# Last stage of a linear attention with a soft mixture of experts: divides on VectorE, chained maxima, sums by halves, 51 weight slots, one written order for the tail

## Chip, cores and metric

The kernel runs on one core of a Trainium2 chip. The metric is the device time of one execution in microseconds; the median of three runs of the kernel before is 335.73 us (335.34 to 335.76). All arithmetic is in float32.

## The reference

Attention without softmax: q, k, v are [8 batches, 8 heads, 576 tokens, 64], and a map `phi` makes 256 positive features of each 64. The result x [4608, 512] goes through a soft mixture of 8 experts with 4 slots each (32 slots).

```python
def phi(x):
    proj = np.einsum('bhsd,df->bhsf', x, w_phi)
    proj = proj - np.max(np.abs(proj), axis=-1, keepdims=True)
    return np.concatenate([np.exp(proj), np.exp(-proj)], axis=-1)
q_p, k_p = (phi(q), phi(k))
kv = np.einsum('bhsf,bhsd->bhfd', k_p, v)
z = np.sum(k_p, axis=2)
num = np.einsum('bhsf,bhfd->bhsd', q_p, kv)
den = np.einsum('bhsf,bhf->bhs', q_p, z)[..., None] + 1e-06
x = num / den                        # then [tokens, heads * 64]
logits = x @ phi_moe                 # [4608, 32]
d = softmax(logits, over tokens);  c = softmax(logits, over slots)
slot_input = d.T @ x                 # [32, 512]
for e in range(8):                   # 4 slots each: 512 -> 1024 -> 512
    slot_out[e] = np.maximum(slot_input[e] @ w1[e], 0.0) @ w2[e]
return c @ slot_out                  # [4608, 512]
```

(Here `phi_moe` is the reference's `phi` of the mixture, and the two softmaxes are written short.)

## The kernel before

**Work and stages.** The batches are taken in 4 pairs of 1152 tokens, 9 tiles of 128 tokens; a pair and a head make a unit (32 units, `NU`), and a unit has 3 chunks of 3 tiles. For each block of 4 tiles TensorE projects q and k (L263), VectorE finds the maxima, ScalarE takes the exponents, and TensorE adds k's features times v into `kvp` (L310). Then `num` (psn, L363) multiplies q's features by it; VectorE scales and adds (L374, L379); POOL adds the denominators (`denom`, L386); VectorE inverts them (L390); POOL divides (`divide`, L405) into tiles of x, `xc` for tiles 0 to 3 and 5 to 8 and `xn` for tile 4 in between. When all heads of a pair are divided, x is transposed on TensorE (psx, L706), copied to SBUF (`xcopy`, L710), and multiplied by the mixture's phi into logits (psl, L416). The maximum over tokens, the sum of exponents (`ssum`) and d.T @ x (`acc`, L455) are kept up as running values, rescaled when the maximum moves.

**The last pair.** Of the last pair, the first three of four column blocks of x are transposed and multiplied ahead (`fturn`, `fxcopy`, `flogits`), and their logits are copied to SBUF (`part`, L728). When the last unit is divided, the rest follows in steps whose names begin with z, for c = 0, 1, 2: transposes (`zturn`, L511) and copies (`zcopy`, L516) of the last column block; `zlog`, which brings `part` back into PSUM by a matmul with the identity (`again`, L422) and adds the last block (L416); `zmax`, a negated maximum (L526) and a minimum with the running one (L528); `zexp` (L534); `zco`, the factors of rescaling (L538); `zlt`, which copies the logits to SBUF for the combine weights (L542); `zdt` and `zde`, which turn the exponents back to tokens (L448, L550); `zsum`, the sums d.T @ x (pss, L558); `zup`, which adds them to `acc` (L563); `zss` for `ssum` (L566, L568); `zone`, the maxima across partitions (L571 to L591); `zst` and `zsi`, which transpose `acc` to the slot inputs `phs` (pst, L601, L603, L606). `zspin` (L613) are four matmuls with constants whose results are not read.

**The tail.** Layer 1 (hp, L813) is followed by `hidden` (L857, L858), `picked` (psh, L866, L869), layer 2 (yp, L888), a copy (`slots`, yt, L895), a matmul that adds the partial sums (`slots2`, psy, L899, and its copy by ScalarE, L900), and the outputs: four matmuls (pso, L908), four copies to `o` by VectorE and ScalarE (L912), two DMAs of 384 KB (L913). `lastw` makes the last three groups' combine weights and `cturn` (L879) transposes all of them.

**What sets the order.** The string `ORDER` names one task after another by a letter; `Plan.run` takes the next task of that kind, and what it issues goes to its engine's queue in that order. In the tail a second string, `TAIL`, sets TensorE's order: L is one layer-2 step (8 matmuls, 16 passes), P `picked`, s `slots`, r `slots2`, O one output group. Layer-2 steps are (q, e): 4 quarters of the columns q, 8 experts e.

**Weights.** 64 tiles of 512 KB (32 of layer 1, 32 of layer 2) come by SP's queue (L234). They lie in slots, whose number grows as pools close: `room` gives 30, 33, 39, 42, 43 and 49 slots. The last 6 of the 49 come with the close of pool "c" (`ends`), which holds x and so waits for `zsum`. The last 15 weights reuse slots of layer 1's weights, and so wait for layer 1.

Of the kernel before, what the change touches and what calls it, by code (L numbers as in the profile page):

```python
# [9 lines left out]
F32 = mybir.dt.float32  # L10
# [8 lines left out]
NBP = B // 2  # L19
# [26 lines left out]
PICK = {'xcopy': 'adda', 'kvcopy': 'daad', 'zcopy': 'ada', 'zlt': 'aadaa', 'zde': 'a'}  # L46
# [75 lines left out]
TAIL = "LLLLLPLLLLLLLsLLLrLsrOLLOLLOLLOLLsOrLLOLLOLLOLLsOrOOO"  # L122
# [3 lines left out]
def tile_kernel(ctx: ExitStack, tc, xT, vv, w, phi, w1, w2, cst, out):  # L126
# [13 lines left out]
    stacks = {k: ExitStack() for k in ("x", "c", "u", "q", "v", "mm", "zl", "num")}  # L140
# [61 lines left out]
    ssum = const.tile([128, 1], F32, name="ssum")  # L202
    low = [const.tile([128, 1], F32, name=f"low{i}") for i in range(2)]
# [177 lines left out]

    def denom(u, t):
        if t[0] == 0:
            dn[u] = sm.tile([128, NT], F32, tag="dn", name="dn", bufs=3)
        t = slice(*t)
        nc.gpsimd.tensor_tensor(dn[u][:, t], qe[u][:, 0, t], un[u][:, t, 64], op=ALU.add)  # L386
# [12 lines left out]
    def divide(u, c):  # L399
# [5 lines left out]
        nc.gpsimd.tensor_tensor(x[:, :, h * D:(h + 1) * D], un[u][:, a:b, 0:64],  # L405
# [12 lines left out]

    def again(ps, p):

        for j in range(G):
            nc.tensor.matmul(ps[32 * j:32 * j + 32], ident[:, 32 * j:32 * j + 32], p, start=True, stop=False, skip_group_check=True)  # L422


# [54 lines left out]
    def wexp(n):  # L479
        nc.scalar.activation(slotw(n), slotw(n), AF.Exp)  # L480
# [27 lines left out]
    def zturn(c):  # L508
        ps = fin["x", c] = zbank("r", ("x", c), [128, G, 128], "psx")
        for j in zj(c):  # L510
            nc.tensor.transpose(ps[:, j], tile4(last_of[c], j)[:, (KC - 1) * 128:KC * 128], ident)  # L511

    def zcopy(c, d):
        t = xTtile(("z", c))
        a, b = zj(c)[0], G
        (nc.vector.tensor_copy if d else nc.scalar.copy)(t[:, a:b], fin["x", c][:, a:b])  # L516
        fin["t", c] = {j: t[:, j] for j in zj(c)}

    def zlog(c):
        ps = fin["l", c] = zbank("lr"[c == 2], ("l", c), [128, 128], "psl")  # L520
        again(ps, part[c])
        slotmm(ps, KC - 1, fin["t", c])

    def zmax(c):
        gm = sm.tile([128, 1], F32, tag="gm", name="gm", bufs=3)
        nc.vector.tensor_reduce(gm, fin["l", c], axis=AX, op=ALU.max, negate=True)  # L526
        lw = sm.tile([128, 1], F32, name=f"lw{c}", bufs=1)
        nc.vector.tensor_tensor(lw, gm, fin["lw", c - 1] if c else low[0], op=ALU.min)  # L528
        fin["lw", c] = lw

    def zexp(c):
        fin["e", c] = sm.tile([128, 128], F32, tag="eT", name="eT", bufs=3)
        fin["s", c] = sm.tile([128, 1], F32, tag="es", name="es", bufs=3)
        nc.scalar.activation(fin["e", c], fin["l", c], AF.Exp, bias=fin["lw", max(c, 1)], accum_out=fin["s", c])  # L534

    def zco(i):
        fin["co", i] = sm.tile([128, 1], F32, tag="co", name="co", bufs=3)
        nc.scalar.activation(fin["co", i], fin["lw", 1] if i else low[0], AF.Exp, scale=-1.0, bias=fin["lw", 1 + i])  # L538
# [14 lines left out]
    def zsum(c):  # L553
        if c != 1:
            fin["sum", c // 2] = zbank("lr"[c == 2], ("s", c), [128, DM], "pss")
        ps = fin["sum", c // 2]
        for j in range(G):
            nc.tensor.matmul(ps[32 * j:32 * j + 32], fin["d", c][:, j], tile4(last_of[c], j), start=c != 1, stop=c > 0,  # L558
                             skip_group_check=True)

    def zup(i, h):
        d = slice(h * DH, (h + 1) * DH)
        nc.vector.scalar_tensor_tensor(acc[:, d], acc[:, d], fin["co", i], fin["sum", i][:, d], op0=ALU.mult, op1=ALU.add)  # L563
# [415 lines left out]
```

## Time and profile before

| | |
|---|---|
| median of 3 runs | 335.73 us (335.34 to 335.76) |
| the profiled execution's own time | 336.97 us |
| its span | 335.2 us |
| granted TensorE clock, 270 to 305 | 1.00 |
| start of layer 1 (hp) | 279.64 |
| first output group (pso) | 305.53 |
| instructions | 16723 |

The profile is of one execution. Its span is what the instructions cover; the execution's own time has 1.77 us more, which lie around it. All positions in the text are microseconds from the start of the span. Rows of a timeline have the start, the length, the engine, the line, the operation, the tiles (out<-in) and how many instructions the row holds; in brackets is how long the engine idled before, and what it waited for ("issue" where the profile shows nothing that it waited for). A busy TensorE in such a row may hold short gaps, as ends of matmuls are modelled.

### The profile page before, as it was taken

What the parts mean: (1) busy time and instruction counts of PE and PEld (TensorE: products, weight loads), DVE (VectorE), ACT (ScalarE), POOL (GpSimd) and SP (SyncE); (2) the same over time, 40 slices, a digit from 0 to 9 for tenths busy, and PEclk for the clock granted to TensorE, in tenths of its full rate; (3) what the DMA queues carried; (4) which work ended last, traced back from release to release, by engine and by line L of the source; (5) the groups of instructions that cost most, each with busy time, mean ns of one, the idle gap of its engine ahead of it and who ended that gap; (6) DMA issues with size and microseconds to landing.
All of it is one profiled execution on the core that took longest, in us unless ns stands there. A gap on an engine that the chain in (4) does not pass through costs nothing.

```text
span 335.2 us, 16723 instructions
## 1 busy us (share of the span) xinstructions
PE 321.5 (96%) x7106; PEld 272.1 (81%) x7106; DVE 239.0 (71%) x682; ACT 228.9 (68%) x676; POOL 162.9 (49%) x344
## 2 busy tenths in 40 slices
PE   8999999999999999899999999999999999999980
PEld 4899999999979999898799999979998843376640
DVE  1478788786979888678898877687898665313560
ACT  2899989967886996788688977867886450002450
POOL 1645785863547667542867687237695310200000
PEclk9999999999999999999999999999999999999997
DMA  6647367563745775464557846225525878997997
GB/s 212 198 130 231 106 210 231 169 226 121 283 167 168 231 275 189 168 231 124 168 202 214 307 157 210 92 60 212 173 103 195 316 311 310 414 407 288 367 372 296
DMA packets 23130, 74.12 MB, mean 221 GB/s; under 512 B 2576, under 2 KB 2960, under 8 KB 23056
## 3 DMA queue, kind: packets, MB, share of 16 engines
q1 hardware_dynamic: 23056, 73.05, 62.1%
q8 instruction: 56, 0.92, 1.1%
q14 instruction: 18, 0.15, 0.1%
HBM read 63.60 MB, written 9.44 MB: 218 GB/s over the span
## 4 chain that ended last, share of the span: by engine, by line
PE 92%; DVE 3%; issue 1%; ACT 1%; DVEq 0%; POOL 0%; ACTq 0%; POOLq 0%
PE kvp L310 23%; PE psn L363 21%; PE psq L263 12%; PE psk L263 11%; PE yp L888 5%; PE psx L706 4%; PE hp L813 4%; PE pso L908 3%; PE psl L416 3%; PE pss L455 2%; PE psw L183 1%; PE pss L558 1%; PE psd L448 1%; PE psh L866 1%; DVE xT L710 1%
## 5 line engine op out<-in xcount | busy, mean ns | idle before, releaser
L283 POOL TENSOR_TENSOR vs<-vt,mk 128x520 f32<-128x520 f32 (+3 forms) x128 | 91.5, 730 | 69.1 <-ACT mk L272 52.1
L310 PE MATMUL kvp<-vs,kf 128*64 128x65 f32 (+1 forms) x2304 | 92.6, 229 | 0.0
L310 PEld LDWEIGHTS kvp<-vs,kf 128*64 128x64 f32 x2304 | 81.5, 138 | 7.2 <-issue 2.3
L363 PE MATMUL psn<-kvs,qf 128*64 128x65 f32 x2304 | 80.1, 223 | 0.1
L263 PE MATMUL psq<-xs,wd 64*128 64x128 f32 x576 | 75.7, 280 | 0.9 <-issue 0.9
L363 PEld LDWEIGHTS psn<-kvs,qf 128*64 128x64 f32 x2304 | 73.4, 138 | 3.1 <-issue 1.0
L263 PE MATMUL psk<-wd,xs 64*128 64x128 f32 x576 | 75.8, 280 | 0.1
L263 PEld LDWEIGHTS psq<-xs,wd 64*128 64x128 f32 x576 | 67.5, 187 | 4.0 <-issue 2.3
L263 PEld LDWEIGHTS psk<-wd,xs 64*128 64x128 f32 x576 | 67.3, 187 | 3.0 <-issue 1.6
L268 DVE TENSOR_REDUCE mk<-psk 128x4 f32<-128x512 f32 x72 | 48.4, 675 | 13.8 <-PE psk L263 8.3
L325 DVE TRANSPOSE_TENSOR_REDUCE mts<-psq 128x16 f32<-128x512 f32 x72 | 50.6, 706 | 6.6 <-PE psk L263 2.9
L294 ACT ACTIVATE kf<-psk 128x512 f32<-128x512 f32 x72 | 42.5, 592 | 17.5 <-DVE mk L268 7.6
L330 ACT ACTIVATE qf<-psq 128x512 f32<-128x512 f32 x72 | 42.3, 594 | 8.8 <-DVE dn L390 3.3
L374 DVE TENSOR_TENSOR un<-psn,eq 128x195 f32<-128x195 f32 x96 | 33.0, 350 | 18.4 <-PE psn L363 9.8
L405 POOL TENSOR_TENSOR xc<-un,dn 128x256 f32<-128x256 f32 x64 | 39.2, 614 | 14.2 <-DVE dn L390 11.8
L333 ACT ACTIVATE qf<-psq 128x512 f32<-128x512 f32 x72 | 43.2, 603 | 0.5 <-DVE mts L325 0.5
L297 ACT ACTIVATE kf<-psk 128x512 f32<-128x512 f32 x72 | 42.6, 596 | 0.5 <-DVE mk L268 0.4
L379 DVE TENSOR_TENSOR un<-psn,un 128x195 f32<-128x195 f32 x96 | 32.8, 349 | 1.0
L341 ACT ACTIVATE mh<-mts 32x36 f32<-32x36 f32 x128 | 29.5, 230 | 4.5 <-DVE mts L325 2.6
L347 DVE TENSOR_REDUCE eq<-mh 32x9 f32<-32x36 f32 x128 | 26.2, 205 | 1.5
L271 ACT ACTIVATE mk<-mk 128x4 f32<-128x4 f32 x72 | 15.2, 210 | 12.4 <-DVE mk L268 10.9
L912 DVE COPY o<-pso 128x384 f32<-128x384 f32 x24 | 12.1, 551 | 9.7 <-PE pso L908 9.7
(116 smaller groups left out, 319.5 us busy)
## 6 DMA issues: line engine op xcount, KB each, us to landing
wt<-w SPq DMA_DIRECT2D x64, 512.0 KB, 6.4
xs<-xT SPq DMA_DIRECT2D x36, 512.0 KB, 4.2
vt<-vv SPq DMA_DIRECT2D x32, 325.0 KB, 3.7
out<-o SPq DMA_DIRECT2D x24, 384.0 KB, 4.4
xs<-xT SPq DMA_DIRECT2D x2, 128.0 KB, 2.6
cs<-cst SPq DMA_DIRECT2D x1, 128.0 KB, 3.1
wd<-w SPq DMA_DIRECT2D x1, 64.0 KB, 2.1
phs<-phi SPq DMA_DIRECT2D x1, 64.0 KB, 2.9
```

What stands on the lines that cost most here:

```text
L263: nc.tensor.matmul(ps, l, r, start=True, stop=True)
L268: nc.vector.tensor_reduce(km[b][:, 2], kx[b], axis=AX, op=ALU.max, apply_absolute_value=True)
L283: nc.gpsimd.tensor_tensor(vs[b][:, :, place(b, u, t, o):place(b, u, t, o) + n], v[:, t + o:t + o + n].unsqueeze(1).broadcast_to([128, 2, n ...
L294: nc.scalar.activation(kf[b][:, 1], kx[b], AF.Exp, scale=-1.0)
L297: nc.scalar.activation(kf[b][:, 0], kx[b], AF.Exp)
L310: nc.tensor.matmul(ps[f:f + FE // 2, pn, o:o + m], kf[b][:, pn, NT * u + t - 4 * b, f:f + FE // 2], v2[:, pn, at:at + m], start=(t == 0 an ...
L325: nc.vector.tensor_reduce(mts.rearrange("p r j -> p j r")[:, o:o + 4], qx[b].rearrange("p j (r t) -> p (j r) t", t=32), axis=AX, op=ALU.ma ...
L330: nc.scalar.activation(qf[b][:, 0], qx[b], AF.Exp)
L333: nc.scalar.activation(qf[b][:, 1], qx[b], AF.Exp, scale=-1.0)
L363: nc.tensor.matmul(ps[64 * f:64 * f + 64, j, pn], q2[:, pn, 64 * f:64 * f + 64], kv[:, pn, b2], start=True, stop=True)
L374: nc.vector.tensor_tensor(un[u][:, CH * c:CH * c + CH], nx[s][:, :, 0], e[:, 1].unsqueeze(2).broadcast_to([128, CH, 65]), op=ALU.mult)
L405: nc.gpsimd.tensor_tensor(x[:, :, h * D:(h + 1) * D], un[u][:, a:b, 0:64], dn[u][:, a:b].unsqueeze(2).broadcast_to([128, b - a, 64]), op=A ...
```

## The change

`divider(u)` gives VectorE instead of POOL for `denom` and `divide` of the last unit. The `again` matmuls and the `zlt` copies are gone: `zmax` is now one `tensor_tensor_reduce`, which writes −(psl + part) over `part` and takes the running minimum along. For chunk 2 it adds a tile of zeros instead, since that chunk's `flogits` go into the very PSUM bank of its `zlog`, with no `part` copy before. Each `zmax` takes the result of the one before it. `zexp` reads `part` with scale −1; chunk 0's exponents use the first minimum, those of chunks 1 and 2 the last. `zzero` clears chunk 1's bank.

`zturn` and `zcopy` of chunk 2 are split in two halves, on ScalarE and VectorE; `zsum` of chunks 1 and 2 goes by halves of 256 columns, each half with its `zup`. The transposed tiles of x get a pool of their own ("t"), which closes after the last `zlog`; the slots are now 30, 33, 39, 42, 43, 45 and 51. `ORDER` is rewritten from its 14th line on. The code of the tail goes inside the manually ordered part for all engines; `lastw` first does the transposes, minima, differences and exponents of all three groups, then their sums and divisions; layer 2 goes quarter by quarter, and `TAIL` is another string.

```diff
-PICK = {'xcopy': 'adda', 'kvcopy': 'daad', 'zcopy': 'ada', 'zlt': 'aadaa', 'zde': 'a'}
+PICK = {'xcopy': 'adda', 'kvcopy': 'daad', 'zde': 'a'}
...
-    "bpzLxAHaArItlmKdknomAfygjvhirwfzAravkdmlhijOgcnowqApAcvbdjmwgsfrfltrlkPymvhijwhajnoxdirkvmgznovjcGpwcblfAdmqlrks"
+    "bpzLxAHaAyrmtdjOGmmfkzIKlhAnigfolcpdvarqbwkghnrldvjAmgivMworwAsfAhtvrxiwvknLcfyhjzAljdocikrjngAwmomvlpNkdbqcfwrg"
...
-TAIL = "LLLLLPLLLLLLLsLLLrLsrOLLOLLOLLOLLsOrLLOLLOLLOLLsOrOOO"
+TAIL = "LLLPLLLLLLsLLrLOLLLOLsLLOrLLOLLOLLsLLrOLLOLLOLLsOrOOO"
...
+    def divider(u):
+
+        return nc.vector if u == NU - 1 else nc.gpsimd
...
-        nc.gpsimd.tensor_tensor(x[:, :, h * D:(h + 1) * D], un[u][:, a:b, 0:64],
+        divider(u).tensor_tensor(x[:, :, h * D:(h + 1) * D], un[u][:, a:b, 0:64],
...
     def zlog(c):
-        ps = fin["l", c] = zbank("lr"[c == 2], ("l", c), [128, 128], "psl")
-        again(ps, part[c])
-        slotmm(ps, KC - 1, fin["t", c])
+        if c == 0:
+            fin["l", c] = zbank("l", ("l", c), [128, 128], "psl")
+        ps = fin["l", c]
+        t = {j: fin["t", c][:, j] for j in zj(c)}
+        for j in t:
+            nc.tensor.matmul(ps[32 * j:32 * j + 32], phs[:, KC - 1], t[j], start=c < 2, stop=True, skip_group_check=True)
...
     def zmax(c):
-        gm = sm.tile([128, 1], F32, tag="gm", name="gm", bufs=3)
-        nc.vector.tensor_reduce(gm, fin["l", c], axis=AX, op=ALU.max, negate=True)
-        lw = sm.tile([128, 1], F32, name=f"lw{c}", bufs=1)
-        nc.vector.tensor_tensor(lw, gm, fin["lw", c - 1] if c else low[0], op=ALU.min)
-        fin["lw", c] = lw
+        lw = fin["lw", c] = sm.tile([128, 1], F32, name=f"lw{c}", bufs=1)
+        if c == 2:
+            part[c] = sm.tile([128, 128], F32, tag="lT", name="part", bufs=3)
+        nc.vector.tensor_tensor_reduce(out=part[c], in0=fin["l", c], in1=zero.broadcast_to([128, 128]) if c == 2 else part[c], scale=-1.0, scalar=fin["lw", c - 1] if c else low[0],
+                                       op0=ALU.add, op1=ALU.min, accum_out=lw)
+        lTs[last_of[c]] = part[c]
...
-        nc.scalar.activation(fin["e", c], fin["l", c], AF.Exp, bias=fin["lw", max(c, 1)], accum_out=fin["s", c])
+        nc.scalar.activation(fin["e", c], part[c], AF.Exp, scale=-1.0, bias=fin["lw", c and 2], accum_out=fin["s", c])
...
+    ZS = (0, 0, 2), (1, 0, 1), (1, 1, 2), (2, 0, 1), (2, 1, 2)
...
-            ("u", [("divide", (NU - 1, 2))]), ("c", [("zsum", 2), ("zlog", 2)])]
+            ("u", [("divide", (NU - 1, 2))]), ("t", [("zlog", c) for c in range(NCH)]), ("c", [("zsum", 4)])]
...
-    last("hopen", 0, None, 0.0, hopen, after=[("zsi", 1)] + [("zspin", i) for i in range(NFIN)] + [("zlt", c) for c in range(NCH)], lat=0.0)
+    last("hopen", 0, None, 0.0, hopen, after=[("zsi", 1)] + [("zspin", i) for i in range(NFIN)], lat=0.0)
...
-        l2 = iter([(q, e) for q, n in ((0, 0), (1, 0), (0, 4), (1, 4)) for e in range(n, n + 4)]
-                  + [(q, e) for q in (2, 3) for e in range(NE)])
+        l2 = iter([(q, e) for q in range(4) for e in range(NE)])
```

The first place is VectorE from the last copies of the last pair to the running minima (`dn` the denominators, `gm` a chunk's negated maximum, `lw` the running minimum, `un` the numerators). Before:

```order
L390 RECIPROCAL dn<-dn 128x3
L516 COPY xT<-psx 128x128
L526 TENSOR_REDUCE gm<-psl 128x1
L528 TENSOR_TENSOR lw_6045<-gm,low_134 128x1
L526 TENSOR_REDUCE gm<-psl 128x1
L528 TENSOR_TENSOR lw_6060<-gm,lw_6045 128x1
L526 TENSOR_REDUCE gm<-psl 128x1
L528 TENSOR_TENSOR lw_6064<-gm,lw_6060 128x1
```

After, in the same place:

```order
L396 RECIPROCAL dn<-dn 128x3
L411 TENSOR_TENSOR xc<-un,dn 128x4x64
L411 TENSOR_TENSOR xn<-un,dn 128x64
L411 TENSOR_TENSOR xc<-un,dn 128x4x64
L531 MEMSET psl 96x128
L519 COPY xT<-psx 128x128
L537 ISA part,lw_6026<-psl,part,low_136 128x128
L537 ISA lw_6026 128x1
L519 COPY xT<-psx 128x256
L575 SCALAR_TENSOR_TENSOR ssum<-ssum,co,es 128x1
L537 ISA part,lw_6045<-psl,part,lw_6026 128x128
L537 ISA lw_6045 128x1
```

The three divides have come from POOL. Each `tensor_tensor_reduce` is two instructions, a wide one and one of 128x1, and between the first and the second minimum now stand the copy of a half of chunk 2 and the first step of `ssum`, which needs chunk 0's sum of exponents and its factor from ScalarE. The third minimum follows the second at once.

The second place is TensorE from the last logits to layer 1 (`psl` logits, `psd` exponents turned back, `pss` sums, `psm` maxima across partitions, `pst` slot inputs, `psw` the spins). Before:

```order
L422 MATMUL psl<-part,cs 32x128 x4
L416 MATMUL psl<-xT,phs 32x128 x4
L448 MATMUL psd<-cs,eT 128x128
L574 MATMUL psm<-cs,lw_6064 1x128
L448 MATMUL psd<-cs,eT 128x128
L558 MATMUL pss<-xc,de 32x512 x4
L582 MATMUL psm<-cs,lr 32x1 x4
L448 MATMUL psd<-cs,eT 128x128
L558 MATMUL pss<-xn,de 32x512 x4
L558 MATMUL pss<-xc,de 32x512 x4
L601 MATMUL pst<-ssum,sf 128x1
L603 MATMUL pst<-sf,acc 128x32 x4
```

After:

```order
L422 MATMUL psl<-xT,phs 32x128 x12
L527 MATMUL psl<-xT,phs 32x128 x4
L447 MATMUL psd<-cs,eT 128x128
L566 MATMUL pss<-xc,de 32x512 x4
L583 MATMUL psm<-cs,lw_6052 1x128
L447 MATMUL psd<-cs,eT 128x128 x2
L566 MATMUL pss<-xn,de 32x256 x4
L591 MATMUL psm<-cs,lr 32x1 x4
L566 MATMUL pss<-xn,de 32x256 x4
L566 MATMUL pss<-xc,de 32x256 x8
L610 MATMUL pst<-ssum,sf 128x1
L612 MATMUL pst<-sf,acc 128x32 x4
```

The 12 first logits of chunk 2 now stand right ahead of its last four, with no identity matmuls between; the two last psd stand together, and the sums go by halves. Two of the spins now follow `pst`.

The third place is TensorE at the first outputs (`yp` layer 2, two rows to a step; `psy` the adding up, `pso` an output group). Before:

```order
L899 MATMUL psy<-yt,cs 128x128
L888 MATMUL yp<-wt_6137,sh 32x128 x4
L888 MATMUL yp<-wt_6139,sh 32x128 x4
L899 MATMUL psy<-yt,cs 128x128
L908 MATMUL pso<-ct,yt 128x384 x4
L888 MATMUL yp<-wt_6141,sh 32x128 x4
```

After:

```order
L908 MATMUL yp<-wt_5843,sh 32x128 x4
L908 MATMUL yp<-wt_5845,sh 32x128 x4
L919 MATMUL psy<-yt,cs 128x128
L908 MATMUL yp<-wt_5847,sh 32x128 x4
L908 MATMUL yp<-wt_5983,sh 32x128 x4
L928 MATMUL pso<-ct,yt 128x384 x4
L908 MATMUL yp<-wt_5985,sh 32x128 x4
```

The first output group had both psy of the first two quarters ahead of it, the second of them right before it; now there is one, with a layer-2 step between it and the group, and twelve steps in all before the first output instead of sixteen.

More of the change, by code (lines that the diff above doesn't have):

```diff
@@ L385, in denom @@
         t = slice(*t)
[L386 removed]
+        divider(u).tensor_tensor(dn[u][:, t], qe[u][:, 0, t], un[u][:, t, 64], op=ALU.add)
     def recip(u, t):
@@ L892, in tile_kernel @@
-    yt = slot(spare[2], "yt").rearrange("p (i q c) -> p i q c", i=2, q=4)
-    def slots(q):
-        nc.vector.tensor_copy(yt[:, 0, q], yp[q])
-    def slots2(q):
-        ps = bank([128, COLS], "psy")
-        nc.tensor.matmul(ps, rep, yt[:, 0, q], start=True, stop=True)
-        return nc.scalar.copy(yt[:, 1, q], ps).ins
-    def outputs(q, g):
-        ps = [bank([128, TRI * 128], "pso") for _ in range(G)]
-        c = ct[g // 2][:, g % 2 * TRI * 128:(g % 2 + 1) * TRI * 128]
-        for j in range(G):
-            rows = slice(32 * j, 32 * j + 32)
-            nc.tensor.matmul(ps[j], yt[rows, 1, q], c[rows], start=True, stop=True)
-        for k in range(2):
-            o = slot(next(free), "o")[:, 0:2 * TRI * 128].rearrange("p (k t) -> p k t", k=2)
-            for j in range(2):
-                (nc.scalar.copy if j else nc.vector.tensor_copy)(o[:, j], ps[2 * k + j])
-            nc.sync.dma_start(out[(q * 3 + g) * 2 + k], o)
@@ new lines, in tile_kernel, with cturn, layer2 @@
+        spare = [order[i] for i in range(len(wsrc) - nslot[-1], len(order)) if order[i] < NE * KC]
+        gone = [i if i < nslot[-1] else order[i - nslot[-1]] for i in range(NE * KC, NE * (KC + 2))]
+        free = iter(spare[3:] + gone + keep[0:2])
+        ct = [slot(spare[i], "ct") for i in range(2)]
+        def cturn(i, a, b):
+            nc.vector.transpose(ct[i][:, 0:(b - a) * 128], call[:, 4 * a:4 * b].rearrange("p t s -> p (t s)"))
+        yp = {}
+        def layer2(q, e):
+            if q not in yp:
+                yp[q] = ph[0].tile([128, 512], F32, tag=f"h{q % 2}", name="yp")[:, 0:COLS]
+            for c in range(FC):
+                g, o = 32 * (c % 4), c % 4 * DH + q % 2 * COLS
+                nc.tensor.matmul(yp[q][g:g + 32], sh[e // 4][:, e % 4, c],
+                                 wt[NE * KC + (q // 2 * NE + e) * 2 + c // 4][:, o:o + COLS],
+                                 start=(e == 0 and c < 4), stop=(e == NE - 1 and c >= 4), skip_group_check=True)
@@ new lines, in tile_kernel, with slots, slots2, outputs @@
+        yt = slot(spare[2], "yt").rearrange("p (i q c) -> p i q c", i=2, q=4)
+        def slots(q):
+            nc.vector.tensor_copy(yt[:, 0, q], yp[q])
+        def slots2(q):
+            ps = bank([128, COLS], "psy")
+            nc.tensor.matmul(ps, rep, yt[:, 0, q], start=True, stop=True)
+            return nc.scalar.copy(yt[:, 1, q], ps).ins
+        def outputs(q, g):
+            ps = [bank([128, TRI * 128], "pso") for _ in range(G)]
+            c = ct[g // 2][:, g % 2 * TRI * 128:(g % 2 + 1) * TRI * 128]
+            for j in range(G):
+                rows = slice(32 * j, 32 * j + 32)
+                nc.tensor.matmul(ps[j], yt[rows, 1, q], c[rows], start=True, stop=True)
+            for k in range(2):
+                o = slot(next(free), "o")[:, 0:2 * TRI * 128].rearrange("p (k t) -> p k t", k=2)
+                for j in range(2):
+                    (nc.scalar.copy if j else nc.vector.tensor_copy)(o[:, j], ps[2 * k + j])
+                nc.sync.dma_start(out[(q * 3 + g) * 2 + k], o)
```

206 lines of the change are left out of this document (101 added, 105 removed), and 4 rows, old and new, of the table LETTERS.

## The prediction

> **What bounds the kernel now.** I read the page first, for the engine that is never free, then the windows view for where that stops being so.
>
> ```profile
> span 335.2 us, 16723 instructions
> PE 321.5 (96%) x7106; PEld 272.1 (81%) x7106; DVE 239.0 (71%) x682; ACT 228.9 (68%) x676; POOL 162.9 (49%) x344
> ```
>
> ```profile
> 250.00:260.00 10.00, 9.95 (x218) 8.88 (x218) 8.42 (x25) 6.88 (x22) 5.81 (x13) 1.00 0.48 172
> 270.00:280.00 10.00, 9.11 (x107) 4.86 (x107) 7.22 (x35) 4.51 (x19) 0.27 (x1) 1.00 0.67 254
> 274.40:277.30 2.90, 2.90 (x33) 0.75 (x32) 2.74 (x16) 1.92 (x9) 0.00 (x0) 1.00 0.09 35
> 277.30:305.40 28.10, 26.25 (x418) 14.79 (x414) 9.31 (x43) 1.95 (x4) 1.85 (x2) 1.00 0.99 389
> 305.40:308.00 2.60, 2.60 (x47) 1.44 (x47) 1.02 (x2) 1.13 (x3) 0.00 (x0) 1.00 0.19 68
> 308.00:333.00 25.00, 17.91 (x313) 10.08 (x310) 11.64 (x24) 9.82 (x24) 0.00 (x0) 0.95 0.97 378
> ```
>
> After the window's length stand the busy times of PE, PE's weight loads, DVE, ACT and POOL, then the granted clock, the DMA share and GB/s. TensorE is full until about 270, so up there only less work on it, or a wait, can move the time. Then comes a stage with short instructions (270 to 280), then the expert weights and the output, where the DMA engines are full but for two holes: 274.4 to 277.3 (share 0.09) and 305.4 to 308 (0.19).
>
> What makes the first hole is seen in the waits and the issues of SP's queue:
>
> ```profile
> SPq L234 <- PE pss L558: 8.1, 1, 8.1
> ```
>
> ```profile
> 276.88 7.78 SPq L234 DMA_DIRECT2D wt<-w  x11
> ```
>
> The next weights wait for the slots that pool "c" holds until the last sums (L558) have run. The second hole lies between the last weight and the first output, which is issued here:
>
> ```profile
> 307.10 23.36 SPq L913 DMA_DIRECT2D out<-o  x24
> ```
>
> From there to the end the outputs fill the DMA (0.97), 24 of them in some 25 us, about 1.0 us each, while TensorE hands them over two at a time. So three things set the end: when layer 1 starts, what TensorE waits for until its first output, and how far the DMA is behind then.
>
> **The change part by part.** The profiled execution took 336.97 us with a span of 335.2, so 1.77 lies around the span; it is 1.24 above the median 335.73 of the runs. I work out a difference against the profiled execution and take it off the median.
>
> The stage before layer 1, in the timeline of all engines (start, length, engine):
>
> ```profile
> 268.34 0.61 POOL L405 TENSOR_TENSOR xc<-un,dn 128x256 f32<-128x256 f32 x1 [0.43 <-DVE dn L390]
> ...
> 269.21 0.86 PE L416 MATMUL psl<-xT,phs 128*32 128x128 f32 x24
> ...
> 269.65 0.62 POOL L405 TENSOR_TENSOR xc<-un,dn 128x256 f32<-128x256 f32 x1 [0.29 <-DVE dn L390]
> ...
> 271.34 0.60 ACT L516 COPY xT<-psx 128x512 f32<-128x512 f32 x1
> ...
> 272.47 0.43 PE L422 MATMUL psl<-part,cs 128*32 128x128 f32 x8
> ...
> 272.71 0.40 PE L416 MATMUL psl<-xT,phs 128*32 128x128 f32 x8
> ...
> 273.51 0.16 DVE L528 TENSOR_TENSOR lw<-gm,lw 128x1 f32<-128x1 f32 x1
> ...
> 273.88 0.30 ACT L538 ACTIVATE co<-low,lw 128x1 f32<-128x1 f32 x1
> ...
> 274.38 0.21 DVE L566 SCALAR_TENSOR_TENSOR ssum<-ssum,co,es 128x1 f32<-128x1 f32 x1
> ...
> 274.90 0.38 ACT L534 ACTIVATE eT<-psl,lw 128x128 f32<-128x128 f32 x1
> ...
> 275.45 0.33 PE L448 MATMUL psd<-cs,eT 128*128 128x128 f32 x1
> ...
> 276.00 0.24 ACT L550 COPY de<-psd 128x128 f32<-128x128 f32 x1
> ...
> 276.60 1.04 PE L558 MATMUL pss<-xc,de 128*32 128x512 f32 x8
> 276.85 1.73 DVE L563 SCALAR_TENSOR_TENSOR acc<-acc,co,pss 128x256 f32<-128x256 f32 x4
> ...
> 279.36 0.36 DVE L606 COPY phs<-pst 128x64 f32<-128x64 f32 x2 [0.32 <-PE pst L603]
> ...
> 279.64 2.81 PE L813 MATMUL hp<-wt,phs 128*32 128x512 f32 x24 [0.32 <-DVE phs L606]
> ```
>
> and, for operations that the trace does not have yet, the groups by form of 262 to 280, whose second number is the mean in ns:
>
> ```profile
> L563 DVE SCALAR_TENSOR_TENSOR acc<-acc,co,pss 128x256 f32<-128x256 f32 x4 | 1.7, 478 | 0.1
> ...
> L710 DVE COPY xT<-psx 128x512 f32<-128x512 f32 x2 | 1.4, 692 | 0.6 <-PE psx L706 0.6
> ...
> L477 DVE TENSOR_TENSOR call<-call,cm 128x128 f32<-128x128 f32 x2 | 0.6, 284 | 0.0
> ```
>
> 1. *Up to the last logits, −0.4.* The last divide of 256 columns takes POOL 0.61; on VectorE I price it between 0.28 (a two-input pass over 128 columns) and 0.48 (a three-operand one over 256), and take 0.42, nearer the second, whose width it has. Two of them stand in the row that the transposes wait for: 2 × (0.61 − 0.42) = −0.4 (−0.7 to −0.3). The last identity step is gone: 272.71 − 272.47 = −0.24; the other two are hidden by the copies that TensorE waits for, so I count nothing. Chunk 2's last copy goes in two halves on two engines: a VectorE copy of 512 columns is 0.69, a half some 0.42 by its share, against the 0.6 of a whole one: −0.2. Against this, the 12 first logits of chunk 2 now stand just before the last four: 24 passes of the row at 269.21 are 0.86, so 0.43. That work was TensorE's ahead of the stage and is only moved, but here it is in the way: +0.4 in this place. Sum −0.4. The two part copies that fall away (of ACT) are hidden.
>
> A page bears on the divide: the Trainium skill, "SBUF — State Buffer", section "SBUF: two separate sides", says that a VectorE instruction with two SBUF inputs and a GpSimd instruction that reads SBUF hold one port pair by turns, and the second waits out the first. No row here shows such a wait; by the page the gain of the divides could be lost while POOL works beside them, and the sum below would be −1.2.
>
> 2. *From the last logits to layer 1, +0.2.* Before, 272.71 to 279.64, 6.93. Four pieces. (a) To the last running minimum: before to 273.67, 0.96. After, the three maxima are a chain, and each is two instructions on VectorE: the wide one lies between 0.28 (L477) and 0.48 (L563), I take 0.36, since one operand is in PSUM but only 128 wide; the narrow one like the row at 273.51, 0.16 to 0.21. Between the first and second stand the half copy and the first ssum step (0.21), which waits for exp (0.38) and co (0.30) on ACT. The second maximum so starts late and the third is done about 1.7 after the last logits: +0.7. (b) From there to the last dispatch weights in SBUF (276.24): before 2.57, since ACT does copies and a co between. After, two exps in a row, one psd, one copy: 0.38 + 0.38 + 0.33 + 0.24 and hand-overs of 0.1: 1.4, so −1.2. (c) Sums: halves let the first half be added while the second runs, but chunk 1 and chunk 2 now come together: +0.1. (d) From acc to layer 1: the second half of pst waits for the first phs copy, and two spin passes stand ahead of layer 1: they lie in TensorE's waits (0.32 at 279.64), and cost up to 0.3 each if these are gone: +0.5 with the pst wait. Sum +0.1; I take +0.2. With VectorE's maxima at their upper price, 0.12 and 0.05 more for three, it would be +0.7; at the lower, 0.
>
> 3. *The rewritten order from about 224 to 268, 0.* TensorE idles 0.05 of 10 us there, so nothing is to be had, only lost. I take nothing, bounds −0.2 and +1.5.
>
> Layer 1 so starts at about 279.4.
>
> 4. *Weight slots.* Two slots come free with the transposed x, ahead of the sums; so two 512 KB weights go in the first hole, and all later ones are earlier by what those two took. At the 389 GB/s of the stretch behind it, two of them are 2.7 us, about the 2.64 us of the hole that are idle (2.90 × 0.91).
>
> 5. *Layer 2 up to the first outputs.* TensorE's rows there:
>
> ```profile
> 301.76 1.95 PE L888 MATMUL yp<-wt,sh 128*32 128x128 f32 x62 [0.83 <-issue]
> ...
> 305.11 0.49 PE L899 MATMUL psy<-yt,cs 128*128 128x128 f32 x2 [0.41 <-DVE yt L895]
> 305.53 0.93 PE L908 MATMUL pso<-ct,yt 32*128 32x384 f32 x8
> 306.39 1.08 PE L888 MATMUL yp<-wt,sh 128*32 128x128 f32 x32
> 307.40 1.66 PE L908 MATMUL pso<-ct,yt 32*128 32x384 f32 x8
> 308.99 1.08 PE L888 MATMUL yp<-wt,sh 128*32 128x128 f32 x32
> ```
>
> The wait of 0.41 for yt goes: the new string puts two layer-2 steps between the copy and its psy. −0.41. The steps themselves are all done in both; the first output comes after 12 of them instead of 16, and one psy is put behind it: with two steps to the row of 1.08, that is 2.2 + 0.49 + 0.41 + 0.2 = 3.3 earlier, at some 302.3, without a gain at the end by itself.
>
> Two rows are longer than their work: 0.83 of "issue" before 301.76, and 1.66 for a pso group that took 0.93 at 305.53, so 0.73. The instruction queue explains both:
>
> ```profile
> q8 instruction: 56, 0.92, 1.1%
> ```
>
> ```profile
> q8 instruction: 1, 0.02, 5.0%
> ```
>
> ```profile
> q8 instruction: 1, 0.02, 4.9%
> ```
>
> The first row is the page's: 56 packets, 0.92 MB, 16 KB each. The others are the DMA view of 299.0 to 300.4 and of 305.4 to 306.8; in the 11 us before the first of these there is none. By count, 2 × 7106 instructions over 56 packets are some 127 passes a packet, and between the two stalls TensorE made 62 + 2 + 16 + 2 + 8 + 32 passes and a few. So each stall is TensorE waiting for its own next block of program, fetched late behind full DMA queues. The first stays where it is: weights still load then. The second comes when, by 4, the weights have been in for some 2.6 us, and its fetch is no longer behind them: −0.73.
>
> The Trainium skill, "Runtime: NRT & Kernel Launch", section "Instruction fetch mechanics", has blocks of 16 KiB, as this trace does, and calls the cost of crossing one "mostly hidden". The 0.83 above disagrees. By that sentence there would be no stall to save and the sum would be −0.9.
>
> 6. *Output phase, −0.3.* From the sixth output group on the two strings are equal, so TensorE has the same work from there. What is different is the queue ahead of the DMA:
>
> ```profile
> out<-o SPq DMA_DIRECT2D x2, 384.0 KB, 4.1
> ```
>
> That is the view of 317.0 to 318.4: 4.1 us to landing, of which two outputs' own share is 2.0. With outputs starting some 3 us earlier this backlog is smaller in the middle; at the end three groups come in a burst in either case, and their landing bounds what is left of it. I take −0.3, between 0 and −1.3.
>
> Sum: −0.4 + 0.2 + 0 − 0.41 − 0.73 − 0.3 = −1.6. The profiled execution would come to about 335.3, the median to 334.1.
>
> **The rivals.**
>
> *The end follows the DMA.* From 277.3 on the DMA is full but for the second hole. If what goes into the first hole comes through in full, the end moves by the 2.6 us of it: 333.1. For it: the shares of 0.99 and 0.97. Against it: after the fifth output group the new string has five layer-2 steps and a psy without an output, 2.5 × 1.08 + 0.49 = 3.2 us, in which the 2 us of an output pair run dry; and TensorE's own work up to its last output is not shortened by earlier weights. 16 in 100.
>
> *The second fetch stays late.* Outputs are already on the queues when TensorE asks for that block, or the packets fall elsewhere, and the 0.73 is lost there or at another place: −0.9, 334.8. For it: both stalls came in less than 8 us, so the place counts. Against it: the second fetch comes well after the weights now. 12 in 100.
>
> *What is gained comes back before layer 1.* The maxima at their upper price (+0.7 instead of +0.2) with ssum waiting for ACT, spins without cover, and that fetch late as well: −1.6 + 0.5 + 0.7 = −0.4, 335.3. For it: VectorE is busy 7.22 of 10 us in that stage and its part of the chain is longer now. Against it: (b) is 1.2 of work that is plainly no longer in the way. 18 in 100.
>
> *Slower: the rewritten order makes TensorE wait between 224 and 268.* Every engine follows its list strictly. In the old one TensorE idles 0.05 us in 250 to 260, while VectorE is at 8.42 and ACT at 6.88 of 10. In 270 to 280, where each step waits for another engine, it idles 0.89 of 10. At 0.6 of that rate, a scale or an exponent that comes late in each round, 44 us lose 4.4 × 0.89 × 0.6 = 2.4, and with the −1.6 the time is 336.5. It decides from 1.6 us of holes on. For it: 0.05 us is no slack, and every piece of the list from there on is in a new place. Against it: the sequence of TensorE's own rows is much the same, and the engines beside it have some 1.5 to 3 us of 10 free. 17 in 100.
>
> **How the numbers follow.** 334.1 stands with 37 in 100. About 0.2%, 0.7 us, is what a measurement of this kernel can tell from no change. Faster: the forecast, the DMA rival and the late fetch, 0.65; within: 0.18; slower: 0.17. The range goes from 332.8, a little below the DMA rival, with divides and backlog at their better ends, to 336.3, which takes in the no-change case and the milder half of the slower one.
>
> **What would show it.** In the profile of the changed kernel: TensorE busy over 9.9 of 10 in 250 to 260 (else the slower rival); layer 1 (hp) starting between 279.0 and 279.8; 1.5 to 2 us from last logits to the last minimum; a DMA share over 0.7 in the 3 us that were at 0.09; no wait for yt before the first outputs; one stall of about 0.8 in layer 2 and no long pso row; first output group at about 302.3. I am wrong if hp starts later than 280, if both stalls are there, or if the end moves by another amount than TensorE's last output group does, save for 0.3.

## The result and the profile after

The changed kernel takes 333.5 us (median of 20 runs, 332.35 to 338.26), the kernel before, timed beside it, 335.44 (20 runs, 334.21 to 339.35). The ratio is 0.9942, 95% interval [0.9921, 0.9963]: −1.95 us, between −2.65 and −1.25. Forecast were −1.6. The profiled execution took 333.26 us, with a span of 331.5.

The span alone is 3.7 us shorter, more than the medians. Part of this is not the change's. TensorE's list is the same in both kernels up to about 223, and yet the two traces are apart there already. This is one group of k times v, in the timeline of TensorE, before and after:

```profile
191.42 1.10 PE L310 MATMUL kvp<-vs,kf 128*64 128x65 f32 x32
```

```profile
190.16 1.10 PE L312 MATMUL kvp<-vs,kf 128*64 128x65 f32 x32
```

The profiled execution of before is 1.26 us late at this place, in a part that the change leaves alone; one wait of 0.87 at 135.04 in it, called "issue", was 0.13 in the other. So I compare distances within a trace: from this mark to layer 1, and from layer 1 to the landing of the last output.

The page of the changed kernel, and its windows, cut where its own DMA share changes (length; busy time of PE, weight loads, DVE, ACT, POOL; clock, DMA share, GB/s):

```profile
span 331.5 us, 16703 instructions
PE 318.7 (96%) x7098; PEld 271.1 (82%) x7098; DVE 240.4 (73%) x688; ACT 229.1 (69%) x674; POOL 161.5 (49%) x339
```

```profile
250.00:260.00 10.00, 9.91 (x242) 9.25 (x239) 9.29 (x30) 8.16 (x24) 7.32 (x19) 1.00 0.53 187
270.00:274.60 4.60, 4.08 (x67) 1.95 (x63) 2.66 (x13) 2.88 (x12) 0.00 (x0) 1.00 1.01 397
274.60:276.60 2.00, 2.00 (x30) 1.25 (x30) 1.35 (x4) 0.29 (x1) 0.00 (x0) 1.00 0.36 100
276.60:301.50 24.90, 24.43 (x359) 12.22 (x361) 10.31 (x47) 2.57 (x6) 1.84 (x2) 1.00 1.01 392
301.50:302.90 1.40, 1.40 (x52) 1.20 (x52) 1.00 (x2) 0.86 (x2) 0.00 (x0) 1.00 0.29 111
302.90:328.70 25.80, 19.45 (x369) 11.65 (x366) 11.83 (x25) 9.99 (x25) 0.00 (x0) 0.93 0.95 368
```

TensorE hardly starves in the rewritten order (9.91 of 10). The first hole of the DMA has shrunk from 2.6 idle us to 1.3 (2.00 × 0.64), the second from 2.1 to 1.0. In the outputs the share is 0.95, with a dip to 0.55 from 313 to 315, behind the four layer-2 steps without an output that start at 310.16.

Up to layer 1, in the timeline of all engines of the changed kernel:

```profile
264.34 0.92 PE L365 MATMUL psn<-kvs,qf 128*64 128x65 f32 x24
...
269.48 0.29 DVE L519 COPY xT<-psx 128x128 f32<-128x128 f32 x1 [2.04 <-PE psl L527]
269.69 0.34 DVE L537 CUSTOM_DVE_ANT_0 part<-psl,part,low 128x128 f32<-128x128 f32 x1
...
269.96 0.08 DVE L537 DVE_READ_ACCUMULATOR2_ANT lw<- 128x1 f32 x1
...
270.27 0.37 ACT L519 COPY xT<-psx 128x256 f32<-128x256 f32 x1 [1.28 <-PE psl L527]
...
270.67 0.40 ACT L544 ACTIVATE eT<-part,lw 128x128 f32<-128x128 f32 x1
270.70 0.20 PEld L527 LDWEIGHTS psl<-xT,phs 128*32 128x32 f32 x8
270.70 0.47 PE L527 MATMUL psl<-xT,phs 128*32 128x128 f32 x8
...
271.38 0.22 DVE L575 SCALAR_TENSOR_TENSOR ssum<-ssum,co,es 128x1 f32<-128x1 f32 x1 [0.69 <-ACT co L548]
...
271.90 1.06 PE L566 MATMUL pss<-xc,de 128*32 128x512 f32 x8 [0.36 <-ACT de L556]
...
272.29 0.08 DVE L537 DVE_READ_ACCUMULATOR2_ANT lw<- 128x1 f32 x1
...
278.13 3.21 PE L833 MATMUL hp<-wt,phs 128*32 128x512 f32 x28
```

From the mark to layer 1 it is 87.97 (278.13 − 190.16) where it was 88.22: −0.25. The last minimum is there 1.67 after the last logits (272.29 + 0.08 − 270.70), as forecast.

TensorE in layer 2 and at the first outputs:

```profile
295.50 3.70 PE L908 MATMUL yp<-wt,sh 128*32 128x128 f32 x128
299.13 0.49 PE L919 MATMUL psy<-yt,cs 128*128 128x128 f32 x2
299.55 0.42 PE L908 MATMUL yp<-wt,sh 128*32 128x128 f32 x7
300.12 0.49 PE L908 MATMUL yp<-wt,sh 128*32 128x128 f32 x9 [0.15 <-issue]
300.54 0.93 PE L928 MATMUL pso<-ct,yt 32*128 32x384 f32 x8
301.40 1.52 PE L908 MATMUL yp<-wt,sh 128*32 128x128 f32 x48
302.85 0.93 PE L928 MATMUL pso<-ct,yt 32*128 32x384 f32 x8
303.70 1.52 PE L908 MATMUL yp<-wt,sh 128*32 128x128 f32 x48
305.15 0.93 PE L928 MATMUL pso<-ct,yt 32*128 32x384 f32 x8
```

The yt wait is gone, every pso group takes 0.93, and of the two waits of 0.83 and 0.73 a single one of 0.15 is left. The first output group stands 22.41 after layer 1 started, where it was 25.89. From layer 1 to the last landing (330.53; before, 334.24) it is 52.40 instead of 54.60: −2.20. With the −0.25 ahead of it that is −2.45, inside the interval of the times.

### The profile page after: what moved, and what is told of

It is laid out like the page before. It is cut to its first block, busy times and chain, and to the rows that moved or that the text cites. A ratio compares the mean times of both kernels' runs of the same rounds, so it can differ in the third digit from the quotient of the medians.

```text
span 331.5 us, 16703 instructions
## 1 busy us (share of the span) xinstructions
PE 318.7 (96%) x7098; PEld 271.1 (82%) x7098; DVE 240.4 (73%) x688; ACT 229.1 (69%) x674; POOL 161.5 (49%) x339
## 4 chain that ended last, share of the span: by engine, by line
PE 93%; DVE 2%; ACT 1%; issue 1%; POOL 0%; DVEq 0%; POOLq 0%; ACTq 0%
PE kvp L312 23%; PE psn L365 21%; PE psq L265 12%; PE psk L265 11%; PE psx L717 5%; PE yp L908 5%; PE hp L833 4%; PE pso L928 3%; PE psl L422 2%; PE pss L454 2%; PE psw L183 1%; PE pss L566 1%; PE psh L886 1%; PE psd L447 1%; PE psy L919 1%
## 5 line engine op out<-in xcount | busy, mean ns | idle before, releaser
L411 POOL TENSOR_TENSOR xc<-un,dn 128x256 f32<-128x256 f32 x62 | 38.1, 616 | 11.5 <-DVE dn L396 8.2
```

Source lines behind the costliest of these rows:

```text
L411: divider(u).tensor_tensor(x[:, :, h * D:(h + 1) * D], un[u][:, a:b, 0:64], dn[u][:, a:b].unsqueeze(2).broadcast_to([128, b - a, 64]), op= ...
```

## The experiments

All are changes of one of the two kernels. Times of a run scatter by some 1 us either way, so a ratio says little below 0.3%. The distances in the traces are finer, but each is from one execution. Against the one trace of before, the two distances together (mark to layer 1, layer 1 to last landing) come out 0.3 to 1.4 us better than the times in every kernel, and outside the interval of the times in three: −1.73 for after_49slots, −2.19 for before_newtail_2fewer, −2.62 for after_pooldivide. So the tail in that trace of before may be longer than usual, and comparisons among the other kernels are the safer ones. "Mark" is the same place of k times v as above; "num" is the start of the last num matmul.

| kernel | ratio to before, 95% | mark to layer 1 | num to layer 1 | layer 1 to last landing |
|---|---|---|---|---|
| before | 1 | 88.11 | 12.49 | 54.60 |
| changed | 0.9942 [0.9921, 0.9963] | 87.86 | 13.09 | 52.40 |
| before_newtail | 0.9997 [0.997, 1.0024] | 88.10 | 12.48 | 53.91 |
| after_oldtail | 0.9991 [0.9968, 1.0013] | 87.71 | 13.09 | 54.02 |
| after_49slots | 0.9984 [0.9953, 1.0014] | 87.87 | 13.09 | 53.11 |
| before_2fewer | 1.0007 [0.9976, 1.0039] | 88.72 | 12.48 | 53.95 |
| before_newtail_2fewer | 0.9975 [0.9944, 1.0007] | 88.05 | 12.48 | 52.47 |
| after_pooldivide | 0.9954 [0.9926, 0.9981] | 87.74 | 13.11 | 52.35 |
| after_zsslate | 0.9947 [0.9924, 0.997] | 88.05 | 13.10 | 52.52 |
| after_xt5 | 0.9936 [0.991, 0.9962] | 87.61 | 12.65 | 52.52 |
| after_xt5_zsslate | 0.9921 [0.9896, 0.9945] | 87.21 | 12.65 | 52.54 |

(The mark here is the 1701st pass of k times v, a few passes into the row above. The distance from num is compared among kernels with the same order only, since the changed order puts other work behind the last num.)

### The tail alone: before_newtail

```diff
-TAIL = "LLLLLPLLLLLLLsLLLrLsrOLLOLLOLLOLLsOrLLOLLOLLOLLsOrOOO"
+TAIL = "LLLPLLLLLLsLLrLOLLLOLsLLOrLLOLLOLLsLLrOLLOLLOLLsOrOOO"
...
+    l2 = iter([(q, e) for q in range(4) for e in range(NE)])
```

> The kernel before with the new tail string and the new order of layer 2 alone; stages ahead of it, weight slots and divides as before. My theory (the gain is the yt wait, plus program blocks whose fetch is no longer behind weights, plus a little ahead of layer 1) expects the yt wait of 0.41 gone and the first output group some 3 us earlier, but the weights end as late as before, so that one late block of about 0.7 stays: -0.4 to -0.7 us against before. The rival that the DMA alone sets the end expects 0.0, since the weights end at the same time and all outputs come behind them. The rival that the tail's order is the whole change expects -1.9.

Measured: −0.1 us, between −1.0 and +0.8, and a distance 0.69 shorter. The yt wait is gone, the first output group comes 3.2 earlier from layer 1 on, and both late waits are there, shown by TensorE's rows:

```profile
302.34 0.65 PE L888 MATMUL yp<-wt,sh 128*32 128x128 f32 x16 [0.62 <-issue]
...
308.35 0.93 PE L908 MATMUL pso<-ct,yt 32*128 32x384 f32 x8 [0.75 <-issue]
```

The tail's order is not the whole change. The time does not tell 0 from −0.7; the distance does.

### The old tail in the changed kernel: after_oldtail

The two edits of before_newtail, the other way round, in the changed kernel.

> The changed kernel with the old tail string and the old order of layer 2. My theory: the gain ahead of layer 1 (0.3) stays, the yt wait of 0.4 is back, the first late block is back at 0.8 as no psy stands ahead of it, the second stays away since the weights end earlier: -0.9 us against before (-0.5 to -1.2). DMA alone: -1.9, as the two weights still go early. Tail alone: 0.

Measured: −0.3 us (−1.1 to +0.4), the distance 54.02, 0.58 below before. The yt wait is back, and the first late block too; no second one:

```profile
301.61 1.73 PE L908 MATMUL yp<-wt,sh 128*32 128x128 f32 x55 [0.60 <-issue]
...
304.75 0.49 PE L919 MATMUL psy<-yt,cs 128*128 128x128 f32 x2 [0.41 <-DVE yt L915]
```

With −0.40 ahead of layer 1 (mark) this is −1.0 in the trace, where my theory had −0.9; the interval of the times takes that in. That the DMA alone sets the end falls: the weights were early and the end was not.

### The slots alone: after_49slots

```diff
-    stacks = {k: ExitStack() for k in ("x", "c", "t", "u", "q", "v", "mm", "zl", "num")}
+    stacks = {k: ExitStack() for k in ("x", "c", "u", "q", "v", "mm", "zl", "num")}
...
+    tp = ctx.enter_context(tc.tile_pool(name="tp", bufs=1, side="right"))
     cp = pool("c", "cp", bufs=BUFS["xc"], side="right")
-    tp = pool("t", "tp", bufs=1, side="right")
...
-            ("u", [("divide", (NU - 1, 2))]), ("t", [("zlog", c) for c in range(NCH)]), ("c", [("zsum", 4)])]
+            ("u", [("divide", (NU - 1, 2))]), ("c", [("zsum", 4)])]
```

(`room` is that of before, and one letter of the order, the close of "t", is left out.)

> The changed kernel without the early close of the transposed tiles' pool: 49 slots, so no weight goes into the hole before the last sums. My theory: the weights end some 2 us later, the block fetch that follows them is late again by about 0.7, and the rest stays: -1.2 us against before (-0.8 to -1.5). DMA alone: 0.0. Slots without effect: -1.9.

Measured: −0.5 us (−1.6 to +0.5), the distance 53.11, 0.71 above the changed kernel. The last weight lands 27.97 after layer 1 started instead of 26.43. The first wait is 0.33 instead of 0.15, and the second is back, half as long as I had it:

```profile
300.34 0.49 PE L908 MATMUL yp<-wt,sh 128*32 128x128 f32 x9 [0.33 <-issue]
...
305.37 1.29 PE L928 MATMUL pso<-ct,yt 32*128 32x384 f32 x8
```

The second stands inside the row, 1.29 instead of 0.93. The two waits make 0.54 of the 0.71; the rest lies between the last burst of output groups and the last landing. The first is not clearly the slots' doing: it is 0.24 to 0.27 in three of the other kernels with 51 slots. So the slots are worth up to 0.7 in the traces, and neither 0 nor all.

### Two transfers fewer, with the old and the new tail

```diff
             i = len(wt)
+            if i > 61:
+                wt.append(wt[i - 2])
+                continue
             t = slot(i if i < nslot[-1] else order[i - nslot[-1]], f"wt{i}")
```

> The kernel before without the last two of the 64 weight transfers; layer 2 uses the two tiles ahead of them in their place, so part of the result is left out. Nothing else is changed, so this is the weights ending two transfers earlier, by itself. My theory: the first late block of layer 2 stays (weights still come then), the second, at pass 6795, is no longer late, the yt wait of 0.41 stays: layer 1 to the last landing 0.7 us shorter than the 54.6 of before, -0.7 us in time. DMA alone: the outputs come two transfers earlier too, -2.5 us.

> The same with the new tail string and the new order of layer 2. My theory: the tail string can hand over outputs some 3 us earlier only to a DMA that is done with the weights, and its late block goes too; so both parts together give what neither gives alone: layer 1 to the last landing 2.0 to 2.3 us shorter than before, as in the changed kernel (52.4), -2.0 us in time. The rival that the two parts just add: the 0.7 us of the tail alone and the gain of the two fewer transfers, so -1.4 us.

Measured: with the old tail the distance is 53.95, −0.65; with the new one 52.47, −2.13. TensorE's rows of the first and of the second:

```profile
300.70 1.95 PE L891 MATMUL yp<-wt,sh 128*32 128x128 f32 x62 [0.62 <-issue]
...
304.05 0.49 PE L902 MATMUL psy<-yt,cs 128*128 128x128 f32 x2 [0.41 <-DVE yt L898]
```

```profile
303.08 0.64 PE L891 MATMUL yp<-wt,sh 128*32 128x128 f32 x16 [0.40 <-issue]
```

So fewer bytes by themselves take the second wait away, and the tail by itself the yt wait; each also shortens the first wait from 0.83 to 0.62. Both together give what the changed kernel has. In the sum of the parts, −0.65 − 0.69 = −1.34, some 0.8 is missing, which the two have only in common. Most of it lies behind TensorE's work. From layer 1 to the start of the last burst of output groups, each part alone gains 0.94 and both gain 1.98, nearly the sum. From there to the last landing it takes 10.54 before, 10.84 with fewer transfers, 10.79 with the tail and 10.39 with both: alone, each part loses 0.25 to 0.30 of its gain while the outputs go out.

In the times the two kernels are +0.2 (−0.8 to +1.3) and −0.8 (−1.9 to +0.2): the first bears out that the outputs do not come earlier just because the weights do, the second is nearer to the −1.4 of the rival than to my −2.0, which lies a little outside. The parts alone are −0.1 and +0.2 in the times, so there too the two together give more than their sum, but the intervals do not rule out that they just add. The traces, one of each kernel, decide for me; the times alone would not have.

### Where the late blocks stand: before_shift64

```diff
-NWARM = 11
+NWARM = 6
...
+    for i in range(69):
+        nc.tensor.matmul(ps[:, 0:16], warm[:, 0:128], warm[:, 0:16], start=True, stop=True)
```

> The kernel before with 69 tiny matmuls in place of five of the eleven warm-up matmuls at its start, so that every later instruction of TensorE stands 64 passes further back in the program. My theory, that the waits called issue are TensorE waiting for its next block of program, expects the two waits of layer 2 at the same pass numbers as before (6668 and 6795 from the program's start), so 64 passes earlier in the work: the first among the layer-2 steps some 2 us sooner, the second in the steps ahead of the first outputs. The rival that they belong to a place of the work (a weight that lands late, a full queue) expects them at the same matmuls as before, pass 6732 and 6859.

Measured: of the two waits expected in layer 2 one is there, at pass 6795 from the start of the program; there is none at 6668, and none at 6732 or 6859. TensorE's rows:

```profile
309.86 0.49 PE L901 MATMUL psy<-yt,cs 128*128 128x128 f32 x2
311.50 0.65 PE L890 MATMUL yp<-wt,sh 128*32 128x128 f32 x16 [1.16 <-issue]
312.56 0.49 PE L901 MATMUL psy<-yt,cs 128*128 128x128 f32 x2 [0.41 <-DVE yt L897]
```

It stands behind the first psy, 64 passes sooner in the work than the pass 6795 of before, which was in the second output group. Over all traces, the waits of over 0.1 called "issue" ahead of the last stage and in layer 2 stand at passes 91, 598, 1230, 1611, 2117, 2751, 2877, 3131, 4016, 4773, 5658, 6666 to 6668 and 6795, in kernels with different work at these numbers; the steps between them are 507, 632, 381, 506, 634, 126, 254, 885, and so on, multiples of about 126.5. So they belong to the program's blocks and not to a place of the work. (This kernel's 343.27 us is one run; its start lost other time that I did not follow, and it is not compared.)

### What ends last ahead of layer 1

```diff
# after_pooldivide
-        return nc.vector if u == NU - 1 else nc.gpsimd
+        return nc.gpsimd
# after_zsslate, in ORDER
-YZ39608022+5
+YZ36080922+5
# after_xt5
-BUFS = {'xs': 3, 'kf': 3, 'vs': 2, 'vt': 2, 'qf': 3, 'un': 2, 'xT': 4, 'xc': 2}
+BUFS = {'xs': 3, 'kf': 3, 'vs': 2, 'vt': 2, 'qf': 3, 'un': 2, 'xT': 5, 'xc': 2}
```

> The changed kernel with the last unit's denominators and divides back on POOL. My theory: the three divides take 1.5 us on POOL instead of 0.9 on VectorE, and the transposes behind them come 0.4 to 0.6 later, so layer 1 does: +0.4 us against the changed kernel, -1.4 against before. The rival that ScalarE's row of copies of transposed x is what ends last there: layer 1 at the same time, -1.9.

Measured: from num to layer 1 13.11 against 13.09. The divides are worth nothing. The rival's time holds; that the copies of transposed x end last, and what they wait for, is seen in the rows. In this kernel the last divide ends at 267.84 on POOL, and VectorE's copy still waits 2.75 us, for logits (psl) that free a buffer:

```profile
267.22 0.62 POOL L411 TENSOR_TENSOR xc<-un,dn 128x256 f32<-128x256 f32 x1
...
268.48 0.62 ACT L721 COPY xT<-psx 128x512 f32<-128x512 f32 x1
...
269.59 0.29 DVE L519 COPY xT<-psx 128x128 f32<-128x128 f32 x1 [2.75 <-PE psl L527]
```

> The changed kernel with one letter moved: the first ssum step stands behind the third maximum in VectorE's order instead of ahead of the second, where VectorE idled 0.69 us for the factor from ScalarE. My theory: the last minimum and with it layer 1 come 0.5 to 0.75 us earlier, and the end too: -2.4 us against before. The rival that the chain of ScalarE and TensorE ends last there in any case: layer 1 at the same time, -1.9.

Measured: the last minimum comes 0.8 sooner after the last logits, layer 1 does not come sooner (13.10 from num). VectorE's and TensorE's rows show why: the sums wait for chunk 0's weights (de), as before the edit.

```profile
270.84 0.08 DVE L537 DVE_READ_ACCUMULATOR2_ANT lw<- 128x1 f32 x1
270.84 0.22 DVE L575 SCALAR_TENSOR_TENSOR ssum<-ssum,co,es 128x1 f32<-128x1 f32 x1
...
271.25 1.07 PE L566 MATMUL pss<-xc,de 128*32 128x512 f32 x8 [0.35 <-ACT de L556]
```

> The changed kernel with five buffers for transposed x instead of four (the weights' third step has then 38 slots instead of 39). In the changed kernel the copies of the last transposes wait up to 2.0 us on VectorE and 1.3 on ScalarE for logits that free a buffer, and ScalarE's exponents stand behind such a copy. My theory: layer 1 comes some 0.4 us earlier, -2.3 us against before. The rival that the order of the rest ends last anyway: layer 1 at the same time, -1.9.

> Five buffers for transposed x and the first ssum step behind the third maximum. The ssum step alone brought the last minimum 0.6 us forward and layer 1 not at all, as TensorE's sums stood behind chunk 0's exponents and not behind the maxima. My theory: with the exponents of chunk 0 earlier, both count: layer 1 0.5 to 0.9 us earlier than in the changed kernel, -2.6 us against before. The rival: as with five buffers alone.

Measured: 12.65 from num to layer 1 in both, −0.44. The fifth buffer gives what I expected of it, moving ssum gives nothing on top, so for the second kernel the rival holds. The chunk 1 copy no longer waits for the logits of chunk 0, but for its own transposes:

```profile
268.35 0.29 DVE L519 COPY xT<-psx 128x128 f32<-128x128 f32 x1 [0.43 <-PE psx L513]
```

The best ratio, 0.9921 [0.9896, 0.9945], is that of after_xt5_zsslate; by time it is not told apart from the changed kernel. Its profiled execution took 337.44 us, with a single block wait of 2.93 us at 127.53, so only distances behind that are used.

## Why the prediction was right, point by point

**The whole.** Forecast −1.6, measured −1.95 (−2.65 to −1.25). The direction, the size and the place, mainly the tail and not the stage, were right; several terms were wrong in size and one reason was wrong. That the size fits is in part luck: in the trace the sum is −2.45, with errors in 1 and 2 that cancel and a gain in 5 that the forecast did not have.

**1, up to the last logits.** The price of the divide was right (0.40 and 0.42 in the trace), its worth was not: after_pooldivide shows 0 in place of −0.4. What ends last there is a buffer. The copies of the last transposes wait 2.04 and 1.28 us for one of four tiles of transposed x that a logits step must free, and a fifth tile moves layer 1 (after_xt5). I had followed operations and not buffers. From the mark to the last logits the trace is 0.75 shorter all the same (81.29 to 80.54), where −0.4 was forecast; no run shows which edit gives it.

**2, from the last logits to layer 1.** The third minimum came as late as worked out (1.67). But it is not what the stage waits for: the sums of chunk 0 are first in TensorE's order and wait for chunk 0's exponents, and after_zsslate moved the minima without moving layer 1. Pieces (a) and (b) were priced on a chain that does not end last. From the last logits to layer 1 it takes 7.43 instead of 6.93, +0.50 where +0.2 was forecast. The sum to layer 1, −0.2 forecast and −0.25 measured, agrees, but not for its parts.

**3, the rewritten order.** From 220 to 260, in steps of 10 us, TensorE idles 0.13, 0.09, 0.16 and 0.09, and 0.28 in the 8 us behind: 0.75 in all, where it idles 0.05 before. So TensorE idles some tenths more in the new order, not nothing more, and far less than the 2.4 of the slower rival, which is out.

**4, the slots.** The last weight lands 1.7 us sooner after layer 1's start (26.43 against 28.09), not 2.6: half of the first hole is still there (0.36 from 274.6 to 276.6), as two weights are gone before the sums end. The size is uncertain: over the traces it lands 24.90 to 27.11 after layer 1 started with 51 slots, and 27.55 to 28.86 with 49 and all the weights.

**5, layer 2.** The yt wait of 0.41 went. The second late block went, −0.73, by the reason given: with two transfers fewer it goes too, with late weights it stays (0.75). The traces' DMA records show the fetch itself: the 16 KB packet for pass 6795 starts 41 and 48 passes ahead of it in before and before_newtail, 56 ahead in after_49slots, where the wait is 0.36, and 75 to 112 ahead in the other eight kernels of the table, which have no wait there.

The first did not stay at 0.83, it fell to 0.15: this step, "the first stays where it is", was wrong, and it is the 0.68 that the forecast lacked. It is 0.60 to 0.83 with the old tail, however early the weights are; with the new tail 0.62 in before_newtail, 0.40 with two transfers fewer, and 0.33 or less in the changed kernel and its variants. Its block comes no sooner. In every trace of the table that has this wait TensorE goes on 21.9 to 22.2 us after layer 1 started, with the old tail and the new, with early weights and late (301.76 − 279.64 = 22.12 before, 300.12 − 278.13 = 21.99 in the changed kernel). What changed is the work ahead of it. With the new tail a psy of 0.42 stands there: the tail alone brings 0.83 to 0.62, and 0.62 to 0.40 with two transfers fewer. In the changed kernel eight passes fewer stand ahead of layer 1, so seven more of layer 2 come before the wait (the x7 in the rows above). Fewer transfers alone bring 0.62 too, with a block that comes 0.2 sooner; whether that is the weights or scatter stays open, as it comes at 22.07 to 22.11 in three kernels with early weights.

The page that calls this crossing mostly hidden (the Trainium skill, "Runtime: NRT & Kernel Launch", "Instruction fetch mechanics") is right for most of the 56 blocks of before, which show no wait of over 0.1, and not for the three that do (0.87, 0.83 and 0.73).

**6, the output phase.** −0.15 from the last burst of output groups to the last landing (10.54 to 10.39), forecast −0.3.

**The rival that the end follows the DMA** falls with after_oldtail and before_2fewer: earlier weights with the old tail bring −0.58 and −0.65 of the 2.20. One argument against this rival had a wrong count: between the fifth and the sixth output group the new string has four layer-2 steps, not five, so 2.65 us without an output (2 × 1.08 + 0.49) and not 3.2.

**The signs named.** Layer 1 starts at 278.13, and at 279.39 with the 1.26 of the mark, as forecast; the yt wait is gone, no pso row is long, and the end moves with the last output groups (−2.20 and −2.06). Two signs failed: the DMA share in the first hole is 0.67 from 273 to 277, not over 0.7, and the one wait left is 0.15, not 0.8. So the first output group comes 0.5 us sooner than the 302.3 named (301.80 with the 1.26).

**The page on the shared port.** In the changed kernel one VectorE denominator of the last unit stands beside a POOL divide, in the timeline:

```profile
262.38 0.62 POOL L411 TENSOR_TENSOR xc<-un,dn 128x256 f32<-128x256 f32 x1
...
262.58 0.43 DVE L392 TENSOR_TENSOR dn<-eq,un 128x3 f32<-128x3 f32 x1
...
266.10 0.17 DVE L392 TENSOR_TENSOR dn<-eq,un 128x3 f32<-128x3 f32 x1
```

The first lasts 0.43 instead of 0.17, and ends when POOL's instruction does (263.01 and 263.00); in the five other traces of this order that have the rows it is 0.43 too. That agrees with the Trainium skill, "SBUF — State Buffer", "SBUF: two separate sides". Here it lies off the path, and the last divides met no work of POOL.

## What to carry to other kernels

Ahead of a chain of short steps, follow the buffers and the order of each queue as well as the operations: here a fifth tile was worth 0.44 us, and three cheaper divides and an earlier maximum nothing. Two edits that each give little alone can be worth most together, so test them alone and together: here earlier weights and an earlier first output, −0.65 and −0.69 alone, −2.1 together, in one trace of each. Before two traces are compared, find a place ahead of the change and take the distance from there; 1.26 of the 3.7 us between these two spans were there already.

## What the runs showed of the hardware

TensorE waits for blocks of its program: at pass numbers that are multiples of about 126.5 apart, whatever the work is there, and from nothing to 2.93 us (at pass 2877 in the trace of after_xt5_zsslate; 0.88 to 1.21 there in three others, and none over 0.1 in the rest). At the first wait of layer 2 it goes on 1.3 to 1.5 us after the 16 KB packet has landed (before: landed at 300.29, on at 301.76; changed: 298.65 and 300.12). The waits ahead of the mark differ from run to run of the same instructions (0.87 and 0.13 at pass 3131), and make up part of the scatter between profiled executions.

The new minimum, one `tensor_tensor_reduce` of 128 x 128, is a row of 0.34 and a read of 0.08, one such pair every 0.5 us (271.52 to 272.02).
